# Moving operands read as words of two halves in turn, with the token order mended where tokens are split

## The chip, the cores and the metric

The kernel runs on one core of one Trainium2 chip. The metric is the device time of one execution in microseconds. Before the change it is 445.85 us, the median of three runs (445.18 to 445.89).

## The reference

An attention block with a polynomial sketch makes 4352 rows of 128 features; a mixture of four experts, each with a hidden layer of 1024, is summed over them with normalised gates. All arrays are float32.

```python
def phi(x):                                   # x: (4, 4, 1088, 32)
    a = np.einsum('rd,bhsd->bhsr', S1, x)     # r = 8
    b = np.einsum('rd,bhsd->bhsr', S2, x)
    return np.einsum('bhsi,bhsj->bhsij', a, b).reshape(*x.shape[:-1], r * r)
q_p, k_p = phi(q), phi(k)
kv = np.einsum('bhsf,bhsd->bhfd', k_p, v)
z = np.sum(k_p, axis=2)
x = (q_p @ kv) / (q_p . z + 1e-6)             # rows (4352, 128) after the heads are joined

p = domain_probs / (domain_probs.sum(-1, keepdims=True) + 1e-09)
for e in range(4):
    h = np.maximum(x @ w1[e], 0.0)            # (4352, 1024)
    out += p[:, e:e + 1] * (h @ w2[e])        # (4352, 128)
```

## The kernel before

The 4352 tokens are cut into ten chunks (`CHUNKS`: 128, 448, six of 512, 320 and 384). In all chunks but the first the tokens lie along the free axis, so they are the moving operand and the columns of the result; the weights are the stationary operand. For each chunk the kernel goes over 4 experts and 8 blocks of 128 hidden units: one such (chunk, expert, block) is a slot. The loop over slots at the end of the function issues, in each slot, the first products of this slot (`opening`), the second products of an earlier one (`second`, five slots later), the closing product of the first layer (`third`), products that were put off (`pay`), and pieces of the attention of later tokens (`piece`), which cost many small matmuls at line 300.

To get float32 accuracy at the rate of the type `F32R`, a number is split into parts, and a product of two numbers is three matmuls. `token_parts` splits the tokens of a chunk: ScalarE makes `xa` (`split`, line 857), VectorE makes `xb` (`join`, line 862), and GpSimd or VectorE makes `xd_` from both (line 926), some slots ahead of their first use. The first layer is then line 1084 (`wa` with `xa`), line 1085 (`wb` with `xb`), a scaling on ScalarE in PSUM (line 1086), and line 1101 (`wd` with `xd_`). ScalarE, VectorE and GpSimd turn the result into the three hidden parts `ha`, `hb` and `hc` (lines 1125 to 1151; the letters in `MAKER` and its kin choose who does what). The second layer is line 1195 (`va` with `ha`), line 1196 (`vb` with `hb`) and, put off to later slots, line 1230 (`vd` with `hc`).

A few blocks are not split. Of chunk 1 the first four blocks ("whole") run in plain F32 in both layers (line 1077, then line 1179), the next twelve ("mixed") only in the second (line 1179). In chunk 1's last two experts block 2 is of kind `X`: its second product is plain F32, at line 1230 (`w_plain`). In the last expert of the last chunk (320 tokens come ahead of it, 384 are in it) two blocks of kind `X` end at line 1233 in plain F32, and two blocks of kind `T` are made by ScalarE (line 1112) and weighted by GpSimd (line 1113), which at the same time writes them in the order of tokens (`by_token`, `by_block`), because line 1276 takes them as stationary operands. `last_sums` (lines 1265 and 1267, VectorE) puts the other sums of that chunk in the same order, and line 1279 adds them.

Before the change every moving operand of these lines is read word after word. The results are columns in the same order as the words of the moving operand.

Of the kernel before, what the change touches and what calls it, by code (L numbers as in the profile page):

```python
# [8 lines left out]
F32 = mybir.dt.float32  # L9
# [15 lines left out]
def kernel(  # L25
# [835 lines left out]
    def join(out, in0, scale, in1, op):  # L861
        nc.vector.scalar_tensor_tensor(out=out, in0=in0, scalar=scale, in1=in1, op0=ALU.mult, op1=op)
# [50 lines left out]

    xparts = {}

    def token_parts(m):

        n = CHUNKS[m]
        t = xpieces("xs", F32R)
        xa, xb, xd_ = (t[:, i] for i in range(3))  # L920
        ((x, _, _),) = placed(START[m], n)
        split(xa[:, 0:n], x, R12)
        join(xb[:, 0:n], xa[:, 0:n].bitcast(F32), 4096.0, x, ALU.subtract)
        xparts[m] = xa, xb, xd_
        yield
        (nc.gpsimd if XD_BY[m] == "P" else nc.vector).tensor_tensor(
            out=xd_[:, 0:n], in0=xa[:, 0:n].bitcast(F32), in1=xb[:, 0:n].bitcast(F32), op=ALU.add
        )
        yield
# [121 lines left out]
    def opening(i):  # L1051

        kind, m, e, k = slots[i]
        n = CHUNKS[m]
        if kind == "pair":
            hd = plain_tile()
            hid[i] = hd
            if i in begun_hp:
                hp = begun_hp.pop(i)
                half_columns(i, hp, HP)  # L1060
            elif i in made_hp:
                hp = made_hp.pop(i)
            else:
                hp = psum(ps_h, "h")
                for j in range(2):
                    both(
                        hp[:, n * j : n * j + n],
                        raw(w1_of, e, 2 * k + j),
                        x_first[:, :],
                        start=True,  # L1070
                        stop=True,
                    )
            nc.scalar.activation(hd[:, 0 : 2 * n], hp[:, 0 : 2 * n], ACTF.Relu)
        elif kind == "whole":
            ((x, _, _),) = placed(START[m], n)
            hp = psum(ps_h, "h")[:, 0:n]
            nc.tensor.matmul(hp, raw(w1_of, e, k), x, start=True, stop=True)  # L1077
            hid[i] = plain_tile()[:, 0:n]
            nc.scalar.activation(hid[i], hp, ACTF.Relu)
        else:  # L1080
            g = psum(ps_h, "h")[:, 0:n]
            w = slice(P * k, P * (k + 1))
            xa, xb, xd_ = (x[:, 0:n] for x in xparts[m])
            nc.tensor.matmul(g, wa[:, e, w], xa, start=True, stop=False)  # L1084
            nc.tensor.matmul(g, wb[:, e, w], xb, start=False, stop=True)  # L1085
            nc.scalar.activation(g, g, ACTF.Copy, scale=1.0 + R12)  # L1086
            begun.append((i, g, wd[:, e, w], xd_))

# [7 lines left out]
    def third(upto):  # L1096

        while begun and begun[0][0] < upto:
            i, g, w, x = begun.pop(0)
            _, m, e, b = slots[i]  # L1100
            nc.tensor.matmul(g, w, x, start=False, stop=True, skip_group_check=True)  # L1101
            n = g.shape[-1]
            if plain_block(m, e, b):
                hid[i] = plain_tile()[:, 0:n]
                if maker(m, e, b) == "Y":
                    nc.vector.scalar_tensor_tensor(
                        out=by_token(hid[i], n), in0=by_block(g, n), scalar=0.0,
                        in1=by_block(gate[m, e], n), op0=ALU.max, op1=ALU.mult,
                    )
                elif maker(m, e, b) == "T":  # L1110
                    above = plain_tile()
                    nc.scalar.activation(above[:, 0:n], g, ACTF.Relu)
                    nc.gpsimd.tensor_tensor(
                        out=by_token(hid[i], n), in0=by_block(above, n), in1=by_block(gate[m, e], n), op=ALU.mult
                    )
                else:
                    nc.scalar.activation(hid[i], g, ACTF.Relu)
                continue
            ha = mpool.tile([P, CW], F32R, tag="ha", bufs=HA, name="ha")[:, 0:n]
            hb = mpool.tile([P, CW], F32R, tag="hb", bufs=HB, name="hb")[:, 0:n]  # L1120
            hc = mpool.tile([P, CW], F32R, tag="hc", bufs=HC, name="hc")[:, 0:n]
            high, rest, both_ = ha.bitcast(F32), hb.bitcast(F32), hc.bitcast(F32)
            by = maker(m, e, b)
            if by not in "DQ":
                nc.scalar.activation(ha, g, ACTF.Relu, scale=NEAR)  # L1125
            if by in "AD":
                nc.scalar.activation(hc, g, ACTF.Relu, scale=NEAR * R12)  # L1127
            if by in "DQ":
                nc.vector.tensor_scalar(out=ha, in0=g, scalar1=0.0, scalar2=NEAR, op0=ALU.max, op1=ALU.mult)
            if by == "S":  # L1130
                nc.scalar.activation(hc, high, ACTF.Copy, scale=R12)
            nc.vector.scalar_tensor_tensor(out=hb, in0=g, scalar=0.0, in1=high, op0=ALU.max, op1=ALU.subtract)  # L1132
            if by == "V":
                nc.vector.scalar_tensor_tensor(out=hc, in0=high, scalar=-R12, in1=rest, op0=ALU.mult, op1=ALU.add)  # L1134
            elif by in "NWZ":
                whole = plain_tile()[:, 0:n]
                if by == "N":
                    nc.scalar.activation(whole, high, ACTF.Copy, scale=1.0 + R12)
                elif by == "Z":
                    nc.vector.scalar_tensor_tensor(  # L1140
                        out=whole, in0=high, scalar=1.0 + R12, in1=g, op0=ALU.mult, op1=ALU.bypass
                    )
                else:
                    nc.gpsimd.tensor_scalar(
                        out=whole, in0=high, scalar1=1.0 + R12, scalar2=1.0, op0=ALU.mult, op1=ALU.mult
                    )
                nc.vector.scalar_tensor_tensor(out=hc, in0=g, scalar=0.0, in1=whole, op0=ALU.max, op1=ALU.subtract)
            else:
                if by in "PQ":
                    nc.gpsimd.tensor_scalar(out=hc, in0=high, scalar1=R12, scalar2=1.0, op0=ALU.mult, op1=ALU.mult)  # L1150
                nc.gpsimd.tensor_tensor(out=hc, in0=rest, in1=both_, op=ALU.subtract)  # L1151
            hid[i] = ha, hb, hc
# [3 lines left out]
    def second(i):  # L1156
# [19 lines left out]
            if k == NP - 1:  # L1176
                weigh(m, e, o)
        elif kind in ("whole", "mixed"):
            nc.tensor.matmul(o[:, 0:n], raw(w2_of, e, k), hd, start=(k == 0), stop=(k == FB - 1))  # L1179
            if k == FB - 1:  # L1180
                owed.append([0, m, e, o, [], ()])
        elif kind == "one":
# [3 lines left out]
            if plain_block(m, e, k):  # L1186
                at = DM * (FB - 1 - k)
                rows = w2_tail[:, at : at + DM] if final(m, e) else w2_plain[m, e][:, 0:DM]
                if maker(m, e, k) in "YT":
                    weighted.append((rows, hd))  # L1190
                else:
                    later.insert(len(later) if final(m, e) else 0, (rows, hd))
            else:
                ha, hb, hc = hd
                nc.tensor.matmul(o[:, 0:n], va[:, w], ha, start=(k == first_of(m, e)), stop=False)  # L1195
                nc.tensor.matmul(o[:, 0:n], vb[:, w], hb, start=False, stop=(k == last))  # L1196
                later.append((vd[:, w], hc))
            if final(m, e):
                if k == last:
# [19 lines left out]
    def pay():  # L1219

        for r in list(owed):
            age, m, e, o, passes, dealt = r
            r[0] += 1
            if not passes:
                continue
            count = dealt[min(age, len(dealt) - 1)] if i < len(slots) or final(m, e) else len(passes)
            for _ in range(min(count, len(passes))):
                w, h = passes.pop(0)
                if not final(m, e):
                    nc.tensor.matmul(o, w, h, start=False, stop=True, skip_group_check=True)  # L1230
                    continue
                opened.append(i)
                nc.tensor.matmul(o, w, h, start=(len(opened) == 1), stop=True, skip_group_check=True)  # L1233
                if len(opened) == FB - MAKER_TAIL.count("Y") - MAKER_TAIL.count("T"):
                    last_sums(m, e, o)
                    owed.remove(r)
# [21 lines left out]

    def by_block(t, n):
        return t[:, 0:n].rearrange("p (g j w) -> p g j w", w=32, g=P // 32)  # L1260

    def last_sums(m, e, o):

# [242 lines left out]
```

## Time and profile before

| | |
|---|---|
| Median of three runs | 445.85 us |
| The profiled execution: its own time | 445.26 us |
| The profiled execution: span, first to last instruction | 443.5 us |
| Busy PE / ACT / POOL / DVE | 436.1 / 392.7 / 357.5 / 356.3 us |
| Granted TensorE clock | 1.00 |
| Matmul instructions | 2820 |

PE is TensorE's matmuls and PEld its weight loads, ACT is ScalarE, DVE is VectorE, POOL is GpSimd. Times of instructions are those of one profiled execution. Matmuls overlap: a matmul's own duration (392 ns for 512 columns) is longer than the time from its start to the start of the next one, and it is this second time that counts for a stream of them. An instruction of ScalarE or VectorE overlaps the next one too, by 0.1 us or less.

### The profile page before, as it was taken

Reading aid. Unit: us, or ns where it says so; the run is one execution under the profiler, and the core shown is the slowest. Engines: PE = TensorE matmul, PEld = TensorE weight load, DVE = VectorE, ACT = ScalarE, POOL = GpSimd, SP = SyncE. Lnnn points to the kernel's source line nnn. Section 1 sums busy time; section 2 is a strip of 40 time slices with the busy share of each in tenths; the row PEclk is TensorE's granted clock in tenths of the full one; section 3 lists DMA queues with packets and bytes.
Section 4 is the critical chain, followed back from the end, with each engine's and each line's share of the span. In section 5 each row is a group of like instructions: output and inputs, shape, how many; then the busy total and the mean of one; then the engine's idle time right before and its main releaser. Section 6 shows DMA issues by size and latency. Waiting matters only on the chain.

```text
span 443.5 us, 8779 instructions
## 1 busy us (share of the span) xinstructions
PE 436.1 (98%) x2820; PEld 357.9 (81%) x2820; DVE 356.3 (80%) x617; ACT 392.7 (89%) x835; POOL 357.5 (81%) x373
## 2 busy tenths in 40 slices
PE   8999999999999999999999999999999999999996
PEld 7876777878778877878878887877787888999995
DVE  5969889787898796887789797796797778787874
ACT  4368898989989997989989997998999999999992
POOL 5443569997999698986899698886899888899891
PEclk9999999999999999999999999999999999999999
DMA  8906230551602204532402412422501120130100
GB/s 242 299 9 176 58 98 1 131 160 46 179 27 70 77 24 111 109 94 74 134 25 58 95 24 79 93 47 62 146 24 36 27 74 16 25 84 20 33 19 18
DMA packets 45453, 34.65 MB, mean 78 GB/s; under 512 B 21728, under 2 KB 38496, under 8 KB 45408
## 3 DMA queue, kind: packets, MB, share of 16 engines
q1 hardware_dynamic: 45312, 34.00, 29.1%
q8 instruction: 22, 0.36, 0.3%
q14 instruction: 23, 0.19, 0.2%
q10 hardware_dynamic: 96, 0.10, 0.1%
HBM read 28.94 MB, written 5.15 MB: 77 GB/s over the span
## 4 chain that ended last, share of the span: by engine, by line
PE 94%; ACT 2%; DVE 2%; DMA 1%; issue 1%; SPq 0%; ACTq 0%; DVEq 0%
PE h L1084 14%; PE h L1101 14%; PE o L1230 13%; PE h L1085 13%; PE o L1195 13%; PE o L1196 13%; PE h L300 7%; PE o L1179 3%; PE o L300 2%; PE h L478 1%; DMA kn<-in_k_dram 1%; PE h L1077 1%; PE h L1233 0%; ACT ring L51 0%; ACT hc L1127 0%
## 5 line engine op out<-in xcount | busy, mean ns | idle before, releaser
L1151 POOL TENSOR_TENSOR hc<-hb,hc 128x512 fp32r<-128x512 f32 (+3 forms) x209 | 260.4, 1264 | 37.5 <-DVE hb L1132 25.8
L1132 DVE SCALAR_TENSOR_TENSOR hb<-h,ha 128x512 fp32r<-128x512 f32 (+3 forms) x266 | 167.9, 642 | 62.4 <-ACT hc L1127 33.4
L1086 ACT ACTIVATE h<-h 128x512 f32<-128x512 f32 (+3 forms) x284 | 162.8, 573 | 5.6 <-PE h L1085 4.9
L1125 ACT ACTIVATE ha<-h 128x512 fp32r<-128x512 f32 (+3 forms) x255 | 146.1, 573 | 5.1 <-PE h L1101 1.2
L1101 PE MATMUL h<-xs,wd 128*128 128x512 f32 (+3 forms) x284 | 113.0, 398 | 1.2 <-ACT h L1086 1.2
L1084 PE MATMUL h<-xs,wa 128*128 128x512 f32 (+3 forms) x284 | 109.4, 385 | 0.0
L1085 PE MATMUL h<-xs,wb 128*128 128x512 f32 (+3 forms) x284 | 106.7, 376 | 0.0
L1195 PE MATMUL o<-ha,va 128*128 128x512 f32 (+3 forms) x266 | 100.3, 377 | 0.0
L1196 PE MATMUL o<-hb,vb 128*128 128x512 f32 (+3 forms) x266 | 100.1, 376 | 0.0
L1230 PE MATMUL o<-hc,vd 128*128 128x512 f32 (+3 forms) x262 | 83.6, 381 | 0.0
L1127 ACT ACTIVATE hc<-h 128x512 fp32r<-128x512 f32 (+3 forms) x134 | 76.8, 573 | 0.0
L1101 PEld LDWEIGHTS h<-xs,wd 128*128 128x128 f32 x284 | 53.3, 188 | 15.3 <-ACT h L1086 3.5
L1084 PEld LDWEIGHTS h<-xs,wa 128*128 128x128 f32 x284 | 53.5, 188 | 13.7 <-issue 3.5
L1150 POOL TENSOR_SCALAR hc<-ha 128x512 fp32r<-128x512 f32 (+3 forms) x75 | 51.0, 680 | 13.7 <-ACT ha L1125 5.9
L1085 PEld LDWEIGHTS h<-xs,wb 128*128 128x128 f32 x284 | 53.5, 188 | 9.1 <-issue 0.6
L1230 PEld LDWEIGHTS o<-hc,vd 128*128 128x128 f32 x262 | 48.6, 188 | 11.0 <-issue 1.6
L1195 PEld LDWEIGHTS o<-ha,va 128*128 128x128 f32 x266 | 50.0, 188 | 9.0 <-DVE total L1330 0.2
L1196 PEld LDWEIGHTS o<-hb,vb 128*128 128x128 f32 x266 | 50.0, 188 | 8.9 <-DVE hb L1132 0.2
L1134 DVE SCALAR_TENSOR_TENSOR hc<-ha,hb 128x512 fp32r<-128x512 f32 (+2 forms) x41 | 40.0, 975 | 2.0
L1204 ACT ACTIVATE o<-o 128x512 f32<-128x512 f32 (+3 forms) x33 | 17.8, 539 | 0.0
L1330 DVE TENSOR_TENSOR total<-o,total 128x512 f32<-128x512 f32 (+3 forms) x26 | 16.9, 651 | 0.9
L1329 DVE TENSOR_TENSOR o<-o,gate 128x512 f32<-128x512 f32 (+3 forms) x26 | 16.9, 649 | 0.5 <-PE o L1230 0.4
(159 smaller groups left out, 400.2 us busy)
## 6 DMA issues: line engine op xcount, KB each, us to landing
w_sb<-in_moe_w_dram SPq DMA_DIRECT2D x8, 512.0 KB
gate<-gates SPq DMA_DIRECT2D x16, 256.0 KB
kn<-in_k_dram SPq DMA_DIRECT2D x4, 544.0 KB
vn<-in_v_dram SPq DMA_DIRECT2D x16, 128.0 KB
gate<-gates SPq DMA_DIRECT2D x8, 224.0 KB
qs<-rows SPq DMA_DIRECT2D x6, 288.0 KB
qs<-rows SPq DMA_DIRECT2D x12, 144.0 KB
qn<-in_q_dram SPq DMA_DIRECT2D x3, 544.0 KB
```

What stands on the lines that cost most here:

```text
L1084: nc.tensor.matmul(g, wa[:, e, w], xa, start=True, stop=False)
L1085: nc.tensor.matmul(g, wb[:, e, w], xb, start=False, stop=True)
L1086: nc.scalar.activation(g, g, ACTF.Copy, scale=1.0 + R12)
L1101: nc.tensor.matmul(g, w, x, start=False, stop=True, skip_group_check=True)
L1125: nc.scalar.activation(ha, g, ACTF.Relu, scale=NEAR)
L1127: nc.scalar.activation(hc, g, ACTF.Relu, scale=NEAR * R12)
L1132: nc.vector.scalar_tensor_tensor(out=hb, in0=g, scalar=0.0, in1=high, op0=ALU.max, op1=ALU.subtract)
L1150: nc.gpsimd.tensor_scalar(out=hc, in0=high, scalar1=R12, scalar2=1.0, op0=ALU.mult, op1=ALU.mult)
L1151: nc.gpsimd.tensor_tensor(out=hc, in0=rest, in1=both_, op=ALU.subtract)
L1195: nc.tensor.matmul(o[:, 0:n], va[:, w], ha, start=(k == first_of(m, e)), stop=False)
L1196: nc.tensor.matmul(o[:, 0:n], vb[:, w], hb, start=False, stop=(k == last))
L1230: nc.tensor.matmul(o, w, h, start=False, stop=True, skip_group_check=True)
```

## The change

Every matmul of these lines reads its moving operand through `halves`: word 0 of the first half, word 0 of the second half, word 1 of the first half, and so on. With 512 columns these neighbours lie 256 words apart. A result's column 2o+i is then the operand's word o of half i. Both layers do this, so the order is changed twice; `token_parts` writes `xa` and `xb` in four quarters, of which quarter b holds the tokens 4a+b, and after both layers the columns of the output are the tokens in order. To do so ScalarE and VectorE read the tokens with a step of four words and write four contiguous runs; `xd_` is made from `xa` and `xb` as before. The four whole blocks of chunk 1 read the tokens themselves: all even ones, then all odd ones (`even_odd`). The kinds `Y` and `T` get new patterns (`to_tokens`, `of_halves`, `of_columns`) since their hidden columns are in another order; only `T` is in use. The first chunk, the attention, `last_sums` and the products at line 1276 and 1279 stay as they are. No instruction is added, removed or moved: on each of the engines the order of instructions is the same in both kernels.

```diff
+    def halves(t):
+        return t.rearrange("p (i o) -> p o i", i=2)
+    def quarters(t):
+        return t.rearrange("p (b a) -> p b a", b=4)
+    def fours(t):
+        return t.rearrange("p (a b) -> p b a", b=4)
+    def even_odd(t):
+        return t.rearrange("p (o i) -> p i o", i=2)
...
     def token_parts(m):
...
-        split(xa[:, 0:n], x, R12)
-        join(xb[:, 0:n], xa[:, 0:n].bitcast(F32), 4096.0, x, ALU.subtract)
+        split(quarters(xa[:, 0:n]), fours(x), R12)
+        join(quarters(xb[:, 0:n]), quarters(xa[:, 0:n].bitcast(F32)), 4096.0, fours(x), ALU.subtract)
...
-            nc.tensor.matmul(hp, raw(w1_of, e, k), x, start=True, stop=True)
+            nc.tensor.matmul(hp, raw(w1_of, e, k), even_odd(x), start=True, stop=True)
...
-            nc.tensor.matmul(g, wa[:, e, w], xa, start=True, stop=False)
-            nc.tensor.matmul(g, wb[:, e, w], xb, start=False, stop=True)
+            nc.tensor.matmul(g, wa[:, e, w], halves(xa), start=True, stop=False)
+            nc.tensor.matmul(g, wb[:, e, w], halves(xb), start=False, stop=True)
...
-            nc.tensor.matmul(g, w, x, start=False, stop=True, skip_group_check=True)
+            nc.tensor.matmul(g, w, halves(x), start=False, stop=True, skip_group_check=True)
...
                     nc.gpsimd.tensor_tensor(
-                        out=by_token(hid[i], n), in0=by_block(above, n), in1=by_block(gate[m, e], n), op=ALU.mult
+                        out=to_tokens(hid[i], n), in0=of_halves(above, n), in1=of_columns(gate[m, e], n), op=ALU.mult
                     )
...
-            nc.tensor.matmul(o[:, 0:n], raw(w2_of, e, k), hd, start=(k == 0), stop=(k == FB - 1))
+            nc.tensor.matmul(o[:, 0:n], raw(w2_of, e, k), halves(hd), start=(k == 0), stop=(k == FB - 1))
...
-                nc.tensor.matmul(o[:, 0:n], va[:, w], ha, start=(k == first_of(m, e)), stop=False)
-                nc.tensor.matmul(o[:, 0:n], vb[:, w], hb, start=False, stop=(k == last))
+                nc.tensor.matmul(o[:, 0:n], va[:, w], halves(ha), start=(k == first_of(m, e)), stop=False)
+                nc.tensor.matmul(o[:, 0:n], vb[:, w], halves(hb), start=False, stop=(k == last))
...
-                    nc.tensor.matmul(o, w, h, start=False, stop=True, skip_group_check=True)
+                    nc.tensor.matmul(o, w, halves(h), start=False, stop=True, skip_group_check=True)
...
-                nc.tensor.matmul(o, w, h, start=(len(opened) == 1), stop=True, skip_group_check=True)
+                nc.tensor.matmul(o, w, halves(h), start=(len(opened) == 1), stop=True, skip_group_check=True)
...
+    def to_tokens(t, n):
+        return t[:, 0:n].rearrange("p (v i g) -> p i g v", i=2, g=P // 32)
+    def of_halves(t, n):
+        return t[:, 0:n].rearrange("p (i g v) -> p i g v", i=2, g=P // 32)
+    def of_columns(t, n):
+        return t[:, 0:n].rearrange("p (g v i) -> p i g v", i=2, g=P // 32)
```

More of the change, by code (lines that the diff above doesn't have):

```diff
@@ L1106, in third @@
                     nc.vector.scalar_tensor_tensor(
-                        out=by_token(hid[i], n), in0=by_block(g, n), scalar=0.0,
-                        in1=by_block(gate[m, e], n), op0=ALU.max, op1=ALU.mult,
+                        out=to_tokens(hid[i], n), in0=of_halves(g, n), scalar=0.0,
+                        in1=of_columns(gate[m, e], n), op0=ALU.max, op1=ALU.mult,
                     )
```

## The prediction

> **What bounds the kernel now.** The page comes first: its engines, and the chain that ended last.
>
> ```profile
> PE 436.1 (98%) x2820; PEld 357.9 (81%) x2820; DVE 356.3 (80%) x617; ACT 392.7 (89%) x835; POOL 357.5 (81%) x373
> ...
> PEclk9999999999999999999999999999999999999999
> ...
> PE 94%; ACT 2%; DVE 2%; DMA 1%; issue 1%; SPq 0%; ACTq 0%; DVEq 0%
> ```
>
> The chain runs through TensorE nearly alone, at the full granted clock. So the time is the sum of TensorE's steps, and the steps are read from starts in the timeline, not from durations. First a slot of 512 columns from the middle, then the last chunk's end (start, duration, engine, line):
>
> ```profile
> 301.62 0.39 PE L1084 MATMUL h<-xs,wa 128*128 128x512 f32 x1
> ...
> 302.78 0.63 PE L1230 MATMUL o<-hc,vd 128*128 128x512 f32 x2
> 303.25 0.40 PE L1084 MATMUL h<-xs,wa 128*128 128x512 f32 x1
> ...
> 435.29 0.69 PE L1233 MATMUL h<-hc,vd 128*128 128x384 f32 x3
> 435.82 1.45 PE L1233 MATMUL h<-hid,w_tail 128*128 128x384 f32 x4
> 437.11 1.50 PE L1276 MATMUL h<-w_tail,hid 128*128 128x128 f32 x12
> ```
>
> Seven split products of 512 columns take 303.25 − 301.62 = 1.63 us, 0.2329 each, or 0.455 ns a column. Three of 384 take 0.53 us, 0.177 each, 0.460 ns a column. So the price goes with the columns, hardly with the count. The plain F32 products behind them are a yardstick: four instructions of 384 take 1.29 us, 0.3225 each, and a plain product is two such instructions (line 1233 has four for its two blocks). If such an instruction is two passes over its columns, a pass costs 0.420 ns a column: less than a split product's single pass, while it needs each word for twice as long. That points to the supply of words at full rate as what costs split products 0.035 ns a column (0.018 us in 512). That it is the supply, and not the mode of multiplication, is inferred.
>
> Next, who else could set the pace. The windows give busy us of PE, PEld, DVE, ACT and POOL in each stretch of 25 us:
>
> ```profile
> 200.00:225.00 25.00, 25.00 (x110) 20.15 (x108) 20.52 (x31) 24.40 (x48) 20.35 (x18) 1.00 0.33 93
> 225.00:250.00 25.00, 25.00 (x145) 20.52 (x144) 21.37 (x40) 23.09 (x48) 22.35 (x21) 1.00 0.32 74
> ...
> 375.00:400.00 25.00, 25.00 (x159) 23.62 (x159) 19.79 (x40) 24.89 (x73) 22.25 (x30) 1.00 0.19 50
> 400.00:425.00 25.00, 24.98 (x143) 23.91 (x142) 20.11 (x36) 24.81 (x63) 22.51 (x27) 1.00 0.12 31
> ```
>
> TensorE has no gap, and ScalarE is next, in the last two windows only 0.1 to 0.2 us behind. TensorE's waits for it are small (in the waits, 1.2 us at line 1101).
>
> **The moving operands.** The change alters how the words of every split product are read, and nothing of how many. By the groups kept apart by shape the split products are 6 × 192 of 512 columns, 126 of 448, 180 of 384 (four of them at line 1233) and 192 of 320: 589,824 + 56,448 + 69,120 + 61,440 = 776,832 columns. At 0.455 ns that is 353 us of the span.
>
> The trace shows no moving operand read with far steps, so the price is bounded from both sides. The best case is a supply that keeps up: 0.420 ns as in the F32 row, a gain of 776,832 × 0.035 ns = 27 us. It would come about if neighbouring words wait for each other in one place of the memory, and words of two places, asked for in turn, get twice the time each. At the other end stands the nearest row with far steps, VectorE's:
>
> ```profile
> L1330 DVE TENSOR_TENSOR total<-o,total 128x384 f32<-128x384 f32 x2 | 1.1, 558 | 0.1
> ...
> L1267 DVE TENSOR_TENSOR hid<-h,total 128x384 f32<-128x384 f32 x1 | 0.9, 852 | 0.0
> ```
>
> Line 1267 writes with a step of four words, line 1330 does the like word after word: 852 against 558 ns, 0.77 ns more a word. On TensorE's columns that is 776,832 × 0.77 ns = 595 us of loss. Between them lies the F32 row again: a word every 0.84 ns (0.3225 us over 384), a pace that TensorE keeps without loss. If far words cost two steps instead of one, the loss is 776,832 × (0.84 − 0.455) = 299 us.
>
> I take the gain. The loss of 0.035 ns is proportional to columns, appears at 512 as at 384, and is gone where words are needed at half the rate; reading two places in turn halves the rate at each. Line 1267 is a write by another engine, and each of its words has a place of its own, whereas `halves` returns to the same two places for several words running.
>
> [...]
>
> **What takes back part of it.** A gain on TensorE is kept only where ScalarE has room. 27 us over the 408 us from the first split product (35 us) to the end is 1.66 us for each 25. Room is 25 minus ScalarE's busy time: from 75 to 425 us the windows leave 3.27, 0.97, 1.66, 3.18, 1.87, 0.60, 1.91, 2.65, 2.15, 0.77, 1.50, 0.63, 0.11 and 0.19. The smaller of 1.66 and the room sums to 16.4 us there; with 2.6 from 35 to 75 and 1.0 in the last stretch, 20 us stay. ScalarE's busy time is an upper bound of what it needs, since its instructions overlap: the truth lies between 20 and 27, near 20 because it works in order and has forced waits. I take 22.
>
> **The token parts.** Nine instructions at line 857 (six of 512, mean 626 ns) and nine at 862 (1064) read with a step of four words. Bounds: nothing, or 852/558, thus 0.3 us on each of ScalarE's, 3 us in all, and 0.56 on each of VectorE's, 5 us. They are issued some slots before use and TensorE waits for none; line 926 starts later by the sum, about 0.9 us at most. Queued behind them are scalings at line 1086 and hidden parts at 1132, which have five slots of lag. What shows is ScalarE's part, at worst 3 us where it has no room: I take 1 us.
>
> **The plain products and the tail.** F32 products (lines 1077, 1179, 1233, `w_plain`) already have two steps for a word: nothing, or, at 0.77 ns a word, 0.34 us for each of 48 instructions, 16 us, which counts only in the slower rival. The two GpSimd instructions at line 1113 (1016 ns each) still write with a step, now eight words, and read the gate two words apart. They end at 436.8 us, line 1276 begins at 437.11: 0.3 us of cover; at 852/558 the pair ends 1.1 us later, and 0.8 us comes on line 1276, of which line 1279 hides 0.2, since it waits for VectorE at 438.8 anyway. I take nothing, at worst 0.6 us.
>
> **Sum.** 445.26 (profiled, 0.6 below the median) − 22 + 1 = 424 us. If ScalarE costs nothing it is 418; if only half of the lower gain comes, and the token parts and the tail cost their worst, it is 445.3 − 10 + 3 + 0.6 = 439.
>
> **Rivals.**
> *Far words cost TensorE a second step (slower).* Each product then paces like an F32 one: 445 + 299 = 744 us; priced by line 1267, 445 + 595 = 1040. [...] It decides as soon as a 512 product starts more than 0.233 us after the last: each further ns costs 1.6 us. TensorE would keep its order, all other engines would idle.
> *Nothing happens.* If the 0.035 ns belongs to the mode of multiplication, or to weight loads beside the stream, the order of words is indifferent, and the token parts hide: 445 to 446 us. For it: weight loads have 81% of the span. Against it: a cost that comes once with a load would not go with the columns (0.455 and 0.460).
> *A partial clash.* The halves of 512, 448, 384 and 320 columns lie 256, 224, 192 and 160 words apart; some distances may fall on one place and cost, others not. At +5% on 353 us that is 463 us, and with the whole widths it joins the first rival.
>
> **Chances.** Faster, with the forecast's 418 to 439 us as its own range: 0.54. Nothing: 0.05 (0.2%, or 0.9 us, is about what a measurement of this kernel tells from no change). Slower: 0.41, of it 0.28 for the second step (0.17 up to 744 us, 0.11 beyond), 0.13 for partial clashes and strided writes on ScalarE's account. The cases have both signs, so the range must reach from 418 to just past 744: 750 leaves out 0.11 above and some 0.02 below.
>
> **What would show it.** Right: the step of a 512 product in the timeline falls from 0.233 to about 0.216 us, F32 products keep 0.3225, ScalarE comes to 95% or more, and PE shows small waits for lines 1086 and 1125 in the last two windows. Line 857 with `xs` above 626 ns would confirm the strided reads. Wrong: a step of 0.233 (nothing), or of 0.43 and more, with PE at 99% and the other engines near half.

## The result, and the profile after

The changed kernel takes 441.64 us (median of four runs, 441.52 to 441.68) against 445.51 us for the kernel before in the same session: a ratio of 0.9913, 95% interval 0.9896 to 0.9931. The change makes the kernel 3.9 us faster; 21 were forecast. The profiled execution took 441.52 us, with a span of 439.7 us.

The page of the changed kernel, its engines and its chain:

```profile
PE 424.3 (96%) x2820; PEld 350.5 (80%) x2820; DVE 364.5 (83%) x617; ACT 393.4 (89%) x835; POOL 359.2 (82%) x373
...
PE 76%; ACT 15%; issue 4%; DMA 2%; DVE 2%; SPq 1%; ACTq 0%; DVEq 0%
```

ScalarE had 2% of the chain before and has 15% now. The timeline of a slot of 512 columns and of the last chunk's end (start, duration, engine, line; the line numbers are 12 to 21 higher than before):

```profile
202.11 0.38 PE L1096 MATMUL h<-xs,wa 128*128 128x512 f32 x1
...
203.19 0.59 PE L1242 MATMUL o<-hc,vd 128*128 128x512 f32 x2
203.62 0.38 PE L1096 MATMUL h<-xs,wa 128*128 128x512 f32 x1
...
431.28 0.65 PE L1245 MATMUL h<-hc,vd 128*128 128x384 f32 x3
431.77 1.78 PE L1245 MATMUL h<-hid,w_tail 128*128 128x384 f32 x4
433.39 1.50 PE L1297 MATMUL h<-w_tail,hid 128*128 128x128 f32 x12
```

Seven split products of 512 columns take 1.51 us, 0.2157 each where it was 0.2329: 0.421 ns a column, the pace hoped for. On 776,832 columns that is (0.455 − 0.421) ns, 26 us gained. These steps are of one slot; the median step of all split products fell from 232 to 216 ns at 512 columns, 204 to 189 at 448, 175 to 163 at 384 and 147 to 136 at 320, which makes 24.6 us, and this is the figure used below. The plain F32 instructions beneath went the other way: four in 1.62 us, 0.405 each, after 0.3225.

Most of the gain is gone again. The waits for the scaling of ScalarE in PSUM (line 1086 before, 1098 after) show where to look, those of TensorE and of its weight loads (in total, times, longest), before and after:

```profile
PE h L1101 <- ACT h L1086: 1.2, 2, 0.8
PEld h L1101 <- ACT h L1086: 3.5, 9, 1.2
```

```profile
PE h L1113 <- ACT h L1098: 7.0, 9, 1.1
PEld h L1113 <- ACT h L1098: 21.5, 48, 1.4
```

Next the tokens' split on VectorE and ScalarE (busy us, mean ns), after and then before:

```profile
L862 DVE SCALAR_TENSOR_TENSOR xs<-xs,ring 128x512 fp32r<-128x512 f32 x6 | 11.3, 1890 | 0.7 <-ACT xs L857 0.7
L857 ACT ACTIVATE xs<-ring 128x512 fp32r<-128x512 f32 x6 | 8.6, 1427 | 0.0
```

```profile
L862 DVE SCALAR_TENSOR_TENSOR xs<-xs,ring 128x512 fp32r<-128x512 f32 x6 | 6.4, 1064 | 0.0
L857 ACT ACTIVATE xs<-ring 128x512 fp32r<-128x512 f32 x6 | 3.8, 626 | 0.0
```

Last, three of the windows after:

```profile
200.00:225.00 25.00, 24.14 (x111) 20.21 (x109) 20.36 (x30) 24.74 (x48) 20.80 (x17) 1.00 0.35 96
225.00:250.00 25.00, 24.96 (x151) 21.54 (x150) 22.43 (x41) 23.98 (x51) 22.70 (x21) 1.00 0.32 70
...
375.00:400.00 25.00, 24.20 (x162) 22.58 (x162) 20.66 (x40) 24.97 (x73) 22.76 (x30) 1.00 0.22 48
```

In the last of them ScalarE (fourth number with a count) went from 24.89 to 24.97 of 25 us, and TensorE from 25.00 to 24.20: it has gaps now. In the timeline, eight of the nine token splits on ScalarE are followed, 0.6 to 1.4 us after their start, by a gap of TensorE of 0.5 to 1.1 us, in which line 1113 waits for line 1098. These eight gaps are 6.1 of the 7.0 us in the row above. A split that took 626 ns takes 1427.

### The profile page after: what moved, and what is told of

Read it like the earlier page. It is cut to its first block, busy times and chain, and to the rows that moved or that the text cites. A ratio compares the mean times of both kernels' runs of the same rounds, so it can differ in the third digit from the quotient of the medians.

```text
span 439.7 us, 8779 instructions
## 1 busy us (share of the span) xinstructions
PE 424.3 (96%) x2820; PEld 350.5 (80%) x2820; DVE 364.5 (83%) x617; ACT 393.4 (89%) x835; POOL 359.2 (82%) x373
## 4 chain that ended last, share of the span: by engine, by line
PE 76%; ACT 15%; issue 4%; DMA 2%; DVE 2%; SPq 1%; ACTq 0%; DVEq 0%
PE h L1113 12%; PE o L1242 11%; PE h L1096 10%; PE h L1097 10%; PE o L1207 9%; PE o L1208 9%; PE h L300 7%; ACT ha L1137 6%; ACT h L1098 5%; PE o L1191 3%; ACT hc L1139 2%; PE o L300 2%; PE h L478 1%; DMA kn<-in_k_dram 1%; PE h L1089 1%
## 5 line engine op out<-in xcount | busy, mean ns | idle before, releaser
L1098 ACT ACTIVATE h<-h 128x512 f32<-128x512 f32 (+3 forms) x284 | 168.1, 592 | 4.7 <-PE h L1097 4.3
L1137 ACT ACTIVATE ha<-h 128x512 fp32r<-128x512 f32 (+3 forms) x255 | 151.4, 594 | 1.5 <-PE h L1113 0.4
L1096 PE MATMUL h<-xs,wa 128*128 128x512 f32 (+3 forms) x284 | 105.5, 372 | 0.0
L1097 PE MATMUL h<-xs,wb 128*128 128x512 f32 (+3 forms) x284 | 102.6, 361 | 0.0
L1207 PE MATMUL o<-ha,va 128*128 128x512 f32 (+3 forms) x266 | 96.7, 364 | 0.3 <-DVE total L1351 0.2
L1208 PE MATMUL o<-hb,vb 128*128 128x512 f32 (+3 forms) x266 | 96.5, 363 | 0.3 <-DVE hb L1144 0.3
L1242 PE MATMUL o<-hc,vd 128*128 128x512 f32 (+3 forms) x262 | 80.2, 368 | 0.5
L1139 ACT ACTIVATE hc<-h 128x512 fp32r<-128x512 f32 (+3 forms) x134 | 79.3, 591 | 0.2 <-DVE hc L1159 0.2
L1146 DVE SCALAR_TENSOR_TENSOR hc<-ha,hb 128x512 fp32r<-128x512 f32 (+2 forms) x41 | 43.7, 1065 | 2.0
L1191 PE MATMUL o<-hid,w_sb 128*128 128x448 f32 x32 | 17.7, 635 | 0.0
```

The costliest lines, as they stand in the source:

```text
L1096: nc.tensor.matmul(g, wa[:, e, w], halves(xa), start=True, stop=False)
L1097: nc.tensor.matmul(g, wb[:, e, w], halves(xb), start=False, stop=True)
L1207: nc.tensor.matmul(o[:, 0:n], va[:, w], halves(ha), start=(k == first_of(m, e)), stop=False)
L1208: nc.tensor.matmul(o[:, 0:n], vb[:, w], halves(hb), start=False, stop=(k == last))
L1242: nc.tensor.matmul(o, w, halves(h), start=False, stop=True, skip_group_check=True)
```

## The experiments

**How the order of words sets the pace.** The first layer's products of the kernel before, with twelve orders of the moving words:

```diff
+    def at_distance(t, w):
+        return t.rearrange("p (o i w) -> p o w i", i=2, w=w)
+    def in_turn(t, i):
+        return t.rearrange("p (i o) -> p o i", i=i)
+    def by_step(t, i):
+        return t.rearrange("p (o i) -> p i o", i=i)
+    def pairs(t, w):
+        return t.rearrange("p (i o w) -> p o i w", i=2, w=w)
...
-            nc.tensor.matmul(g, wb[:, e, w], xb, start=False, stop=True)
+            product(cell(m, e), g, wb[:, e, w], xb, start=False, stop=True)
```

> The kernel before, with only the first layer's split products of the six chunks of 512 reading their tokens in twelve ways (two experts for each), and the plain F32 second products of chunk 1 in four ways; the columns' order is not mended, so this run is for the steps between starts alone. Theory A (two places far apart get twice the time each): 0.216 us from start to start for halves, quarters in turn, and words 64 or 16 apart in turn; 0.233 for plain order, for words 2 apart in turn and for every second word. Theory B (any order in which neighbours are not adjacent words avoids the clash): 0.216 for all but the plain order. [...]

The one execution took 483.16 us. Each order has its own line; the rows for `wb` (busy us, mean ns of one) are, from the top: plain, words 2 apart in turn, 4 apart in turn, halves, four quarters in turn, pairs of words from the halves in turn, every second, every fourth and every eighth word.

```profile
L930 PE MATMUL h<-xs,wb 128*128 128x512 f32 x16 | 6.3, 394 | 0.0
L932 PE MATMUL h<-xs,wb 128*128 128x512 f32 x16 | 6.3, 395 | 0.0
L934 PE MATMUL h<-xs,wb 128*128 128x512 f32 x16 | 6.1, 378 | 0.0
L942 PE MATMUL h<-xs,wb 128*128 128x512 f32 x16 | 6.1, 379 | 0.0
L944 PE MATMUL h<-xs,wb 128*128 128x512 f32 x16 | 7.1, 444 | 0.0
L946 PE MATMUL h<-xs,wb 128*128 128x512 f32 x16 | 8.0, 502 | 0.0
L948 PE MATMUL h<-xs,wb 128*128 128x512 f32 x16 | 10.1, 634 | 0.0
L950 PE MATMUL h<-xs,wb 128*128 128x512 f32 x16 | 10.3, 643 | 0.0
L952 PE MATMUL h<-xs,wb 128*128 128x512 f32 x16 | 9.8, 610 | 0.0
```

A duration is the step from start to start and some 0.16 to 0.18 us more: the medians of the steps are 0.231, 0.231, 0.215, 0.2155, 0.277, 0.330, 0.453, 0.461 and 0.4315 us in the same order. Words 8, 16 and 64 apart in turn step at 0.215 to 0.216 too. So the five orders at full pace, 0.215 to 0.216 us, have two things in common that none of the others has together: neighbours from two different groups of four words, and not more than two such groups in use. It is the order of reading that sets the pace, since nothing else about these products differs between the rows; why two groups are best, no run shows. Theory A had the first half right and put the distance too far (4 words are enough, 2 are not); it missed four quarters (0.277) and every second word (0.453). Theory B falls, as four orders without adjacent neighbours are slower than plain. The slowest are every second, every fourth and every eighth word, at nearly twice the plain step. For plain F32 products of 448 columns the means were 538 ns in plain order, 636 by halves, 555 by every second and 956 by every fourth word: order matters there as well, but plain is the best.

**The tokens' split alone undone, the F32 products alone undone, both undone.** The edits of the second and third run; the fourth has both:

```diff
-        split(quarters(xa[:, 0:n]), fours(x), R12)
-        join(quarters(xb[:, 0:n]), quarters(xa[:, 0:n].bitcast(F32)), 4096.0, fours(x), ALU.subtract)
+        split(xa[:, 0:n], x, R12)
+        join(xb[:, 0:n], xa[:, 0:n].bitcast(F32), 4096.0, x, ALU.subtract)
```

```diff
-            nc.tensor.matmul(hp, raw(w1_of, e, k), even_odd(x), start=True, stop=True)
+            nc.tensor.matmul(hp, raw(w1_of, e, k), x, start=True, stop=True)
...
-            nc.tensor.matmul(o[:, 0:n], raw(w2_of, e, k), halves(hd), start=(k == 0), stop=(k == FB - 1))
+            nc.tensor.matmul(o[:, 0:n], raw(w2_of, e, k), hd, start=(k == 0), stop=(k == FB - 1))
...
-                    nc.tensor.matmul(o, w, halves(h), start=False, stop=True, skip_group_check=True)
+                    nc.tensor.matmul(o, w, h if h.dtype == F32 else halves(h), start=False, stop=True, skip_group_check=True)
```

> The changed kernel with the tokens split in their own order again, so that ScalarE and VectorE read and write without steps (the order of the output's rows is then not mended). Theory T (the split with steps is on the path): line 857 for tokens falls from about 1470 to 625 ns, nine times, 7 us of ScalarE, and the waits of line 1113 for line 1098 that are near 1 us go: 434 to 435 us. Rival S (ScalarE is saturated everywhere, wherever its work lies): less than 3 us come back, 439 us. Rival N (the split is hidden by the slots between it and its use): 441.6.

> The changed kernel with the plain F32 products of chunk 1 and of the last chunk in word order again (columns of chunk 1 not mended). In the changed kernel an F32 instruction of 448 columns takes 0.236 us a pass against 0.187 before. Theory F (TensorE bounds chunk 1, so this is on the path): 16 products by 0.19 us and a few others, 4 us back, 437.7 us. Rival S (ScalarE is the bound there too): under 1 us.

> The last two together: halves only in the split products, tokens split in plain order, F32 products in word order. Theories T and F: 441.6 - 7 - 4 = 430.5 us. Rival S: 436 us or more, with line 1113 still waiting for line 1098 in every chunk, because ScalarE's instructions stand back to back.

Measured 435.88, 437.07 and 431.62 us (ratios to before 0.9800, 0.9785 to 0.9815; 0.9826, 0.9811 to 0.9841; 0.9706, 0.9690 to 0.9722). Against the 441.64 us of the changed kernel the split costs 5.8 us, the F32 products 4.6, and both 10.0. That compares two sessions, in which the kernel before took 445.51 and 444.83 us; by the ratios to it the three are 5.0, 3.9 and 9.2 us. Theories T and F hold, T a little short of its 7 us, and S falls for these two. The F32 products' part is their own time: an instruction of 448 columns steps at 469 ns by halves and 375 in plain order, 3.0 us for 32 of them. With the plain split PE's waits for line 1098 shrink by nearly the gain (7.0 to 1.4 us):

```profile
PE h L1113 <- ACT h L1098: 1.4, 2, 0.9
```

The run undoes the join on VectorE (1890 ns after, 1064 before) together with the split on ScalarE; that the cost is ScalarE's is read from these waits.

**Is the rest ScalarE's?** The scaling of line 1086 (1098 after) on half of its columns, in the kernel before and in the fourth run's:

```diff
-            nc.scalar.activation(g, g, ACTF.Copy, scale=1.0 + R12)
+            nc.scalar.activation(g[:, 0 : n // 2], g[:, 0 : n // 2], ACTF.Copy, scale=1.0 + R12)
```

> The kernel before with line 1086's scaling on half of the columns only (the other half is left unscaled), which takes some 0.2 us from ScalarE in each of 284 slots, near 55 us in all. TensorE bounds the kernel before by itself: 445 falls by 3 us at most (its waits for line 1086 and what hangs on them). If ScalarE already held it back: 435 or less.

> The changed kernel with tokens split in plain order, F32 products in word order (columns not mended), and line 1098's scaling on half of the columns. If the split, the F32 products and ScalarE's queue are all that took the products' 26 us back: 442.0 (the kernel before with the same light scaling) - 26 = 416 us. If it stays above 420 us, a fourth loss is left beside them.

Before with light scaling: 441.99 us (0.9934, 0.9921 to 0.9946), 3.0 less. The fourth run's kernel with light scaling: 420.62 us (0.9452, 0.9436 to 0.9468), 11.0 less than its 431.62. The same relief is worth 3.0 us before the change and 11.0 after it, so some 8 us of the gain had become waits for ScalarE. The waits of the weight loads for line 1098 agree, in the fourth run's kernel and in its light version:

```profile
PEld h L1113 <- ACT h L1098: 16.3, 49, 1.2
```

```profile
PEld h L1113 <- ACT h L1098: 2.1, 5, 1.0
```

Between the two light kernels lie 21.4 of the 24.6 us, so some 3 us are still lost elsewhere. The first line of the light version shows ScalarE below the others:

```profile
PE 410.3 (98%) x2820; PEld 353.9 (85%) x2820; DVE 358.9 (86%) x617; ACT 345.4 (82%) x835; POOL 357.7 (85%) x373
```

What holds those 3 us was not settled. In this kernel's windows TensorE's gaps lie mostly between 45 and 125 us (1.5 us of 80), where GpSimd is at 24.41 of 25 us in one window; but it is at 24.33 in that window of the light kernel before too, where TensorE has no gap. Summed over all split products, the time above the median step is 15.0 us here and 11.6 in the light kernel before, and the difference is spread over all four widths.

**A version that keeps the pace and pays less for the order.** Two neighbouring groups of four words (lines, in the expectations and the code) read in turn, 0.215 us a product in the pattern run, need tokens mixed only within eights, so the split can be two instructions of half the width with short steps. Chunk 1 stays in plain order, the last chunk as in the changed kernel:

```diff
+    def lines_in_turn(t):
+        return t.rearrange("p (o i w) -> p o w i", i=2, w=4)
+    def moving(m, t):
+        return t if m == 1 else halves(t) if m == NC - 1 else lines_in_turn(t)
...
+            orders = [
+                (lambda t, i=i: t.rearrange("p (o w i) -> p i o w", i=2, w=4)[:, i], lambda t, i=i: t.rearrange("p (o i w) -> p i o w", i=2, w=4)[:, i])
+                for i in range(2)
+            ]
+        for to, of in orders:
+            split(to(xa[:, 0:n]), of(x), R12)
+        for to, of in orders:
+            join(to(xb[:, 0:n]), to(xa[:, 0:n].bitcast(F32)), 4096.0, of(x), ALU.subtract)
```

> A version with its columns in order: chunk 1 reads and splits in plain order, chunks of 512 and 320 read two neighbouring lines in turn (words 0, 4, 1, 5, 2, 6, 3, 7 of each eight), which paced 0.215 us in the pattern run, and the tokens are split by two instructions of half the width with short steps instead of one with a step of four words; the last chunk stays as in the changed kernel. Theory TF (what the change lost lies in the strided token split and in chunk 1's F32): 441.6 - 6 - 4 + 2 (chunk 1's split products at their old pace) = 433 to 434 us. Rival S (ScalarE's count of work alone sets the time): 437 or more.

434.80 us, ratio 0.9773 (0.9761 to 0.9786): faster than both kernels, and within 1 us of what theory TF said. With light scaling:

> The version with two lines in turn, with the same half-width scaling. Theory S (after the change ScalarE is the bound that takes the gain back): with ScalarE light the products' pace comes through, 445 - 25 = 420 to 422 us, and TensorE is again without waits. Rival: if it stays within 3 us of the version it is made from, the rest of the gain is lost elsewhere (PSUM banks, VectorE, GpSimd).

426.15 us (0.9574, 0.9560 to 0.9587), 8.7 less, short of the 420 to 422 expected. Of the 8.7 us the kernel before has 3.0 too, so ScalarE is a part of what is left, and not all. TensorE is not without waits either: those for VectorE at its second products are 3.4 us here, after 0.5 without the light scaling.

**Taking work off ScalarE.** First its scaling of the second layer's sums given to VectorE (`O_BY = 'VVVV'`), then two of 32 blocks a chunk given to VectorE or to GpSimd (one of the two new lines in each run):

```diff
-    MAKER_LATE = ('APPVANAA', 'APAVPVAA', 'APPVANPA', 'APVPAADA')
+    MAKER_LATE = ('APPVANVA', 'APAVPVAA', 'APPVANPA', 'APVPAVDA')    # to VectorE
+    MAKER_LATE = ('APPVANPA', 'APAVPVPA', 'APPVANPA', 'APVPAADA')    # to GpSimd
```

> As the version with two lines in turn, and VectorE instead of ScalarE scales the second layer's sums (33 instructions, 0.47 us each by their starts). Theory S (ScalarE is what is left of the loss; VectorE has room): 4 to 8 us less than the version it is made from. Rival V (VectorE, in order, holds the hidden parts up behind the scalings): the same or slower.

> The version with two lines in turn, with two of the 32 blocks of each chunk from 512 on turned from kind A (ScalarE makes a part of hc, GpSimd the rest) to kind V (VectorE makes hc). Per chunk ScalarE has 0.94 us less by its starts, GpSimd 2.6 less, VectorE some 2 more. Theory S: six to eight chunks by 0.5 to 0.9 us, 3 to 6 us faster than 434.8. Rival V (hidden parts come later behind VectorE's queue): same or slower.

> As before this one, but two blocks of each chunk from kind A to kind P: GpSimd makes that part of hc, 0.7 us each, ScalarE has 0.94 us less a chunk. Theory S: 3 to 6 us faster than 434.8. Rival G (GpSimd, near 21 of 25 us busy, becomes late with hc): same or slower.

The scaling on VectorE: 491.18 us (1.1032, 1.1000 to 1.1063). It is slower as rival V said, though at another place: line 1259's put-off products wait for the scaling itself, 44.3 us in 29 waits, and TensorE's busy share is 89% where it was 98% with the scaling on ScalarE:

```profile
PE o L1259 <- DVE o L1235: 44.3, 29, 5.2
```

TensorE's granted clock was 0.97 in this execution, against 0.997 to 1.00 in the other runs.

Blocks to VectorE: 434.59 us (0.9762, 0.9747 to 0.9776), no difference, as rival V said; whether for its reason was not examined. Blocks to GpSimd: 432.98 us (0.9718, 0.9696 to 0.9740), the best of the versions with their columns in order, 1.8 us better where 3 to 6 were expected.

**Does ScalarE pay for the read or for the write?** The changed kernel with the split, and VectorE's join, reading the tokens word after word and writing to four quarters in turn:

```diff
+    def placed_by(t):
+        return t.rearrange("p (b a) -> p a b", b=4)
+    def in_order(t):
+        return t.rearrange("p (a b) -> p a b", b=4)
...
-        split(quarters(xa[:, 0:n]), fours(x), R12)
-        join(quarters(xb[:, 0:n]), quarters(xa[:, 0:n].bitcast(F32)), 4096.0, fours(x), ALU.subtract)
+        split(placed_by(xa[:, 0:n]), in_order(x), R12)
+        join(placed_by(xb[:, 0:n]), placed_by(xa[:, 0:n].bitcast(F32)), 4096.0, in_order(x), ALU.subtract)
```

> The changed kernel with the split of the tokens stepping on its writes instead of its reads: ScalarE and VectorE read the tokens word after word and write to four quarters in turn; VectorE reads xa from four quarters in turn. The result is the same. If ScalarE pays for reading a new line at each word and not for writing one, line 857 falls from 1470 to near 630 ns and the time to 436 or 437 us. If writes with far steps cost the same, 1470 ns and 441.6 us again.

439.24 us (0.9867, 0.9850 to 0.9883). The split's row shows 1154 ns, between the plain 626 and the 1427 with the steps on the read, so ScalarE pays for both, and 2.4 us come back, not 5.8:

```profile
L857 ACT ACTIVATE xs<-ring 128x512 fp32r<-128x512 f32 x6 | 6.9, 1154 | 0.0
```

## Why the prediction was right about the operands and wrong about what takes the gain back

The forecast sum has three terms that take something from the gain. All three came out larger, and a further loss had no term (us):

| Term | Taken | Shown by the runs |
|---|---|---|
| Gain on the moving operands | 27 | 24.6 |
| Lost because ScalarE has no room | 5 | 8 |
| Token parts | 1, at worst 3 | 5.0 to 5.8 |
| Plain F32 products | 0 | 3.9 to 4.6 |
| Elsewhere | 0 | about 3 |
| Left | 21 | 3.9 |

So the step that failed is the price of what takes the gain back: 6 us of 27 were taken off, and some 21 of 24.6 were lost. The plain products were put at nothing, the token parts at a fifth of what they cost, and ScalarE's idle time was read as room that could all be used.

**The moving operands: right.** The forecast step was 0.216 us, the measured one 0.2157; the gain on TensorE's columns was put at 27 us and is 24.6. Its reason was right in part: the order of reading is what cost 0.034 ns a column (0.2329 against 0.2157 us a product). Whether it does so through the supply of words, as the author inferred, no run shows, and "two places" turned out to be two groups of four words in use at a time, however near. The first rival, a second step for far words, did not come at 0.2157 us: `halves` returns to the same two groups for several words running, the difference from line 1267 that the prediction named, and every fourth word, which does not, took 0.461 us. The pattern run shows how near it was. Four quarters in turn would have cost 0.277 us, which the argument of two places did not foresee, and every second word 0.453, close to the rival's F32 pace. That the order chosen was one of the five at full pace was in part luck.

**ScalarE's room: too small a loss, from a wrong reading.** The prediction took 22 of 27 us as kept, from "room is 25 minus ScalarE's busy time". Measured, some 8 us became waits for ScalarE (11.0 less 3.0 by the light runs), and about 3 more are not accounted for. The reading counts every idle moment as room, but part of ScalarE's idle time is a wait that it cannot use: in the kernel before,

```profile
ACT qT L51 <- PE h L300: 10.6, 6, 2.6
```

six times it stands still for attention products while the slots' scalings queue behind. These six waits lie in five of the six windows that seemed to have most room (3.27, 3.18, 2.65, 2.15 and 1.87 us). Without them the prediction's sum over the windows gives 10.6 us in place of 16.4, so some 14 us kept in place of 20. After the change the waits are still there, 9.9 us in six. How much of the 8 us is due to them, no run shows. Nor was the kernel before bound by TensorE alone, as the prediction said: light scaling took 3.0 us off it.

**The token parts: mis-sized.** The prediction took 1 us, at worst 3, with the ratio 852/558 of VectorE's line 1267. Measured: 626 to 1427 ns on ScalarE, over all nine 6.2 us more (11.6 against 5.4), of which 5.0 to 5.8 us came back when it was undone. The row was a write by another engine; reading with steps costs ScalarE 2.3 times. VectorE's join, 1064 to 1890 ns, is above its bound too. The cover named, five slots of lag, did not help: what waits is line 1113, one slot behind line 1098, which stands in ScalarE's queue behind the split.

**The plain products: a cost put at nothing.** F32 products that "already have two steps for a word: nothing" cost 3.9 to 4.6 us. F32 instructions by halves take 0.405 us for 384 columns where plain order took 0.3225: 0.21 ns a word, over a quarter of the 0.77 ns that had been kept for the slower rival alone, and all of it is on the path. The tail cost nothing through GpSimd, as taken: its two instructions (line 1125 after) took 1026 ns each where they had taken 1016.

**Sum.** 24.6 us gained; 9 to 10 lost to split and F32, 8 to ScalarE's queue, about 3 elsewhere: 3.9 us remain. The signs were called right and each cost but the last was named. Two of them were taken from a row of another engine or at nothing, and the third from busy shares.

## What to carry to other kernels

Here one engine was at 98% and the next at 89%, and the faster first engine kept only a part of its gain until the second's queue was relieved. In such a case, read from the waits how much of the second's idle time is itself waiting, and test it with a run that makes its work light. An order that pays on one engine must be made somewhere: price the making on the engine that does it, in the queue where it stands, and look for the smallest permutation that does the job (eights instead of quarters of a chunk were worth 6.8 us here by the medians, together with a chunk left in plain order). And an order that speeds one type of product may slow another, as it did here (`F32R` 232 to 216 ns a step at 512 columns, F32 375 to 469 ns at 448): apply it by type.

## What the runs showed of the hardware

TensorE took 4-byte words of the type `F32R` in plain order at 0.455 ns each, at a granted clock of 1.00 (0.999 in the pattern run). Of the twelve orders tried, those that alternated word by word between two groups of four words reached 0.42 ns: words 4, 8, 16, 64 or 256 apart in turn took 0.215 to 0.216 us for 512. Other orders of 512 took 0.277 us with four groups, 0.330 with pairs from two, and 0.43 to 0.46 with every second, fourth or eighth word. Plain F32 instructions, which took a word every 0.84 ns in plain order (0.3225 us for 384), were slowed by the alternation that helps `F32R`, from 375 to 469 ns a step for 448 columns. ScalarE's read with a step of four words took 2.3 times as long as a plain one (1427 against 626 ns for 512), a write to four places in turn 1.8 times (1154).
